# A split product before the second values half: reordering the opening of each step of a fused attention and feed-forward kernel

## The chip, the cores and the metric

The kernel runs on one core of a Trainium2 chip. The metric is device time in microseconds (us), median of several executions. Medians, ranges and ratios below are of executions of the fast state. Ratios are computed as the mean time of one kernel's fast runs over that of the other's fast runs in the same rounds, so they are not quite the ratios of the medians that are quoted beside them; the interval after a ratio is its 95% interval.

## The reference, cut to what matters

```python
def _attn_ref(q, k, v):                 # 8 batches, 8 heads, 576 tokens, head size 64
    k_p = k.reshape(B, H, Sp, 8, D).mean(axis=3)      # keys and values pooled by 8
    v_p = v.reshape(B, H, Sp, 8, D).mean(axis=3)
    attn = softmax(scale * q @ k_p.T)
    return attn @ v_p
def _moe_ref(x, w_in, w_out):           # x: 4608 x 512, w_in: 512 x 2048
    return gelu_tanh(x @ w_in) @ w_out
```

The output of the attention is the input x of the feed-forward part.

## The kernel before

The kernel works in nine steps: one for 512 tokens of each batch, and one ("the remainder") for the 64 left-over tokens of all eight. While TensorE runs the feed-forward part of step g, the attention of step g+1 is woven into it by "hooks": `at(hooks, s, f, ...)` puts the call of f ahead of the matmul numbered s. The attention of one step runs in this order: scores on TensorE, their exponentials ("exps") on ScalarE, the softmax sums on VectorE, transfers on the sync queue that transpose the result into the tile eT, and the values on TensorE, which are copied into the tile xT. xT is what the first product of the next step reads. Hooks 0 to 63 lie in the first product (w_in), 64 to 175 in the second (w_out).

From the fourth step on both products save work by a Strassen-like scheme. Half of the first product is done with seven quarter products ("split products") of 8 matmuls, 128x256 each; two PSUM tiles, x4 and y4, collect sums of products, and in-between sums (partials k2, k0, k1) are copied out to SBUF while later products go on adding into the same tile. The second product has seven output products of 16 matmuls.

```python
def hidden_fast(g, hook):                            # before; cut
    t1, t2, t3, t4 = x_sums(g)                       # needs all of xT
    hidden_two(g, hook)                              # two plain products, need all of xT
    product(x4, 1, A(0, 0), X(0, 0), 8)              # X(h, c): tokens c to c+255 only
    k2 = osb_tile()...
    nc.scalar.copy(out=k2, in_=x4)
    product(y4, 1, A(1, 0), X(1, 0), 12)
    add(out=k2, in0=y4, in1=k2, op=ALU.add)          # add = VectorE
    hidden(g, 2, hook, 16)
    gelu(0, 0, k2)
    product(x4, 0, S(2), T(t2), 20)
    k0, k1 = k2, spare
    nc.scalar.copy(out=k0, in_=x4)
    product(y4, 1, S(1), T(t1), 24)
    nc.scalar.copy(out=k1, in_=y4)
    ...
```

The tail of a step: output products, with the values (attention times V) of the next step in two halves of 256 tokens.

```python
for n, (prod, acc, fresh) in enumerate([(1,xs,1), (2,y,1), (5,z,1), (6,xs,0), (7,xs,0), (3,z,0), (4,xs,0)]):
    ...   # after 1, 6: ScalarE copies xs out; after 5: k2 += y; after 7: k1 += xs; after 3: k0 += z, then store
at(hooks, 64 + 84,  pool, ..., 5, 9)     # VectorE sums of the next values, behind product 7
at(hooks, 64 + 100, values, n, 0)        # within product 4
at(hooks, 64 + 107, values, n, 1)
def osb_tile():
    return work.tile([128, 2, DM], F32, name="osb")  # two buffers, used in turn
```

The softmax here doesn't subtract the row's maximum and nothing guards it: scores larger than these inputs give would overflow.

Of the kernel before, what the change touches and what calls it, by code (L numbers as in the profile page):

```python
# [8 lines left out]
F32 = mybir.dt.float32  # L9
BF16 = mybir.dt.bfloat16  # L10
ALU = mybir.AluOpType
# [8 lines left out]
def kernel(  # L20
# [21 lines left out]
    nc = tc.nc  # L42
# [10 lines left out]
    R = B  # L53
# [265 lines left out]
    BIG = [(64, 0), (0, 1), (64, 1), (0, 2), (0, 3), (64, 3), (0, 4), (64, 4)]  # L319
    SMALL = [(0, 1), (64, 1), (0, 2), (64, 2), (96, 2), (32, 3), (96, 3), (32, 4)]  # L320

    def values(g, half):

        xo = psum.tile([128, HP, 256], F32, name="xo", tag="sc", bufs=2)
        eT, t0 = st[g]["eT"], 256 * half
        for part, rows_ in ((SMALL, 32), (BIG, 64)):
            for pr in range(HP):
                for hh in range(2):
                    r0, c = part[2 * pr + hh]
                    n = dict(PARTS[pr])[c]  # L330
                    nc.tensor.matmul(out=xo[64 * hh:64 * hh + 64, pr, :],  # L331
                                     lhsT=vbd[r0:r0 + rows_, g, n, 64 * hh:64 * hh + 64],
                                     rhs=eT[r0:r0 + rows_, 2 * half:2 * half + 2, c, :],
                                     start=(part is SMALL and pr % 2 == 0), stop=(part is BIG), skip_group_check=True)
        for i, eng in enumerate((nc.scalar, nc.vector)):
            copy(eng, st[g]["xT"][:, 2 * i:2 * i + 2, t0:t0 + 256], xo[:, 2 * i:2 * i + 2])

    def values_r(g):

        xo = [psum.tile([128, 2, MAIN], F32, name="xo", tag="sc", bufs=2) for _ in range(2)]  # L340
        eT = st[g]["eT"]
        for i in range(2):
            for pr in (2 * i, 2 * i + 1):
                for b in range(B):
                    p0 = 64 * (b % 2)
                    for x, (c, n) in enumerate(PARTS[pr]):
                        nc.tensor.matmul(out=xo[i][:, pr % 2, 64 * b:64 * b + 64], lhsT=vbd[:, b, n, :],
                                         rhs=eT[:, b // 2, c, p0:p0 + 64], start=(x == 0), stop=(x == 1))
            copy((nc.scalar, nc.vector)[i], st[g]["xT"][:, 2 * i:2 * i + 2], xo[i])

    def store(g, r, osb, c0=0, c1=DM, eng=nc.sync):
        if g < B:
# [43 lines left out]
    def osb_tile():  # L396
        return work.tile([128, 2, DM], F32, name="osb")
# [38 lines left out]
    def x_sums(g):  # L436

        tt = work.tile([128, 4, 5, 128], BF16, name="tt", tag="eT", bufs=1)
        t1, t2, t3, t4 = t = [tt[:, i, 0:4, :].rearrange("p (i a) b -> p i (a b)", i=2) for i in range(4)]
        x = st[g]["xT"].rearrange("p (h i) t -> p h i t", h=2)  # L440
        b11, b12, b21, b22 = [x[:, h, :, c:c + 256] for h in range(2) for c in (0, 256)]
        for out, in0, in1 in ((t1, b12, b11), (t2, b22, t1), (t3, b22, b12), (t4, b21, t2)):
            nc.vector.tensor_tensor(out=out, in0=in0, in1=in1, op=ALU.subtract)
        return t

    def hidden_fast(g, hook):

        t1, t2, t3, t4 = x_sums(g)
        y, x = [psum.tile([128, 2, MAIN], F32, name="c2", tag="sc", bufs=2) for _ in range(2)]
        y4, x4 = [c.rearrange("p b (m t) -> p (b m) t", m=2) for c in (y, x)]  # L450
        xt = st[g]["xT"].rearrange("p (h i) t -> p h i t", h=2)
        add = nc.vector.tensor_tensor

        def product(acc, fresh, lhs, rhs, s):
            for m in range(4):
                for i in range(2):
                    if i == 0:
                        hook(s + m)
                    nc.tensor.matmul(out=acc[:, m, :], lhsT=lhs(i, m), rhs=rhs(i), start=bool(fresh and i == 0 and m % 2 == 0),  # L459
                                     stop=(i == 1), skip_group_check=True)  # L460

        def A(h, e):
            return lambda i, m: wi[:, h, i, MQ + m, e, :]

        def S(n):
            return lambda i, m: ws[:, n - 1, i, m, :]

        def X(h, c):
            return lambda i: xt[:, h, i, c:c + 256]

        def T(t):
            return lambda i: t[:, i, :]

        def gelu(e, c, src):
            nc.scalar.activation(out=gq[:, MQ:MQ + 4, e, c:c + 256], in_=src, func=ACT.Gelu_apprx_tanh)  # L475

        hidden_two(g, hook)
        product(x4, 1, A(0, 0), X(0, 0), 8)
        k2 = osb_tile().rearrange("p b (m t) -> p (b m) t", m=2)
        nc.scalar.copy(out=k2, in_=x4)  # L480
        product(y4, 1, A(1, 0), X(1, 0), 12)
        add(out=k2, in0=y4, in1=k2, op=ALU.add)
        hidden(g, 2, hook, 16)
        gelu(0, 0, k2)
        product(x4, 0, S(2), T(t2), 20)
        k0, k1 = k2, spare
        nc.scalar.copy(out=k0, in_=x4)  # L487
        product(y4, 1, S(1), T(t1), 24)
        nc.scalar.copy(out=k1, in_=y4)
        hidden(g, 3, hook, 28)  # L490
        product(x4, 0, S(3), T(t3), 32)
        add(out=k1, in0=x4, in1=k1, op=ALU.add)  # L492
        hidden(g, 12, hook, 36)
        gelu(1, 256, k1)
        product(y4, 0, S(4), X(1, 256), 40)
        add(out=k0, in0=y4, in1=k0, op=ALU.add)
        product(x4, 0, A(1, 1), T(t4), 44)
        gelu(1, 0, x4)
        gelu(0, 256, k0)
        for i, fo in enumerate((13, 14, 15)):  # L500
            hidden(g, fo, hook, 48 + 4 * i)
        for i in range(60, 64):
            hook(i)

# [7 lines left out]
        for f in range(2):  # L512
            nc.scalar.activation(out=gT[:, f, :], in_=hp[f], func=ACT.Gelu_apprx_tanh)

    def mlp(g, hooks, last, fast):
        hook = runner(hooks)
        if fast:
            hidden_fast(g, hook)
        else:
            hidden_two(g, hook)  # L520
            for fo in range(2, FO):
                hidden(g, fo, hook, 4 * fo)
# [28 lines left out]

        add = nc.vector.tensor_tensor
        lhs = {1: (gq, 0, 0), 2: (gq, 1, 0), 4: (gq, 1, 256), 5: (gq, 0, 256)}
        for n, (prod, acc, fresh) in enumerate([(1, xs, 1), (2, y, 1), (5, z, 1), (6, xs, 0), (7, xs, 0), (3, z, 0), (4, xs, 0)]):
            for p in range(2):
                for m in range(NP):
                    hook(64 + 16 * n + 8 * p + m)
# [195 lines left out]
    def tail_of_attention(hooks, n, va):  # L753
        at(hooks, va, xT_tile, n)
        at(hooks, va, nc.scalar.preload_act_table_set, GELU_SET)
        at(hooks, va, values, n, 0)
        at(hooks, va, values, n, 1)

    hooks = {}
    at(hooks, 16, first_t, 2)  # L760
# [45 lines left out]
    for n_, g in enumerate(seq):  # L806
# [4 lines left out]
        if n_ == 1:  # L811
            for i in range(1, 4):
                at(hooks, i, w_sums, i, 0, NP, nc.vector)
            at(hooks, 36, g_sums, 0, 4)
            at(hooks, 57, g_sums, 4, 6)
        elif fast:
            at(hooks, 45, g_sums, 0, 2, (0,))
            at(hooks, 57, g_sums, 2, 6, (0,))
            at(hooks, 65, g_sums, 6, 8, (0,))
            at(hooks, 65, g_sums, 0, 8, (1,))  # L820
        else:
            at(hooks, 20, g_sums, 0, 2)
            at(hooks, 36, g_sums, 2, 4)
            at(hooks, 57, g_sums, 4, 6)
        if not fast:
            at(hooks, 65, g_sums, 6, 8)
        if n_ + 1 < len(seq):
# [16 lines left out]
                at(hooks, t1, spread_v, b, nc.gpsimd)  # L844
                at(hooks, 56, k_spread, b, [nc.vector, nc.vector])
            elif kv:
                at(hooks, 4, pool, b, 0, 5, (0,))
                at(hooks, 16, pool, b, 0, 5, (1,))
                at(hooks, 16, dup_k, b, 0, 5)
                at(hooks, 16, kT_tile, b, None)  # L850
                at(hooks, 16, k_transpose_dma, b)
                at(hooks, 16, spread_gated, b)
                at(hooks, 40, k_spread, b, [nc.gpsimd, nc.gpsimd])
            if fast:
                sc_at = [76, 76, 100, 100]
                norm_at = [84, 88, 106, 106]
            else:
                sc_at = [68, 68, 94, 94]
                norm_at = [81, 97, 104, 114]
            for j in range(4):  # L860
                at(hooks, sc_at[j], scores, n, j)
                at(hooks, sc_at[j], exps, n, j)
            at(hooks, norm_at[0], eT_tile, n)
            if fast:
                for j in (2, 3):
# [2 lines left out]
                at(hooks, norm_at[j], norm, n, j, nc.gpsimd if j == 1 else nc.vector)  # L868
                at(hooks, norm_at[j], e_transpose_dma, n, j)
            at(hooks, 64 + 66, nc.scalar.preload_act_table_set, GELU_SET)  # L870
            if n == R:
                at(hooks, 64 + 105, xT_tile, n)
                at(hooks, 64 + 105, values_r, n)
            else:
                at(hooks, 64 + 100, xT_tile, n)
                at(hooks, 64 + 100, values, n, 0)
                at(hooks, 64 + 107, values, n, 1)
        if n_ + 2 < len(seq):
            n2 = seq[n_ + 2]
# [3 lines left out]
            at(hooks, 64 + 52, cast_gated, n2)  # L883
            if n_ >= 2 and n2 != B - 1:
                at(hooks, 64 + 84, pool, B - 1 if n2 == R else n2, 5, 9)
            at(hooks, 64 + 100, qT_tile, n2)
            at(hooks, 64 + 100, q_transpose_dma, n2)
            if n_ == 1:
                at(hooks, 45, load_kv, n2, (0,))
                at(hooks, 64 + 100, load_kv, n2, (1,))  # L890
            else:
                at(hooks, 28, load_kv, n2)
        mlp(g, hooks, n_ + 1 == len(seq), fast)


# [28 lines left out]
```

## Time and profile before

| | before |
|---|---|
| median | 290.24 us (290.11 to 291.05, 3 runs) |
| profiled execution | 291.53 us, span 289.8 us |
| busy: TensorE, VectorE, ScalarE | 94%, 77%, 62% |
| the steps, between exp table loads | 30.09, 29.42, 30.12, 29.40, 29.84, 29.23 us |

The last row is a handy ruler: ScalarE loads the exp table once in each step, just after the first output product has begun, so the gaps between these loads are step lengths.

Here is the timeline view of the kernel before at the end of a step (start us, length us, engine, line, operation, output and input, count, and in brackets how long the engine had been idle and for whom). L587 is the sum into partial k0 of the second product, the first L402 its store, L480 the copy of the first partial k2 in the next step.

```profile
170.15 0.68 DVE L587 TENSOR_TENSOR osb<-mm,osb 128x512 f32<-128x512 f32 x1
...
170.85 0.36 SPq L402 DMA_DIRECT2D out_dram<-osb  x1
...
174.60 1.01 ACT L480 COPY osb<-c 128x1024 f32<-128x1024 f32 x1 [0.22 <-PE c L459]
```

The store lands about 3.1 us after its issue. The copy, which overwrites the stored buffer, waited only for its matmuls (PE).

### The profile page before, as it was taken

The numbers are of one execution on the slowest core, as the hardware profiler recorded it, in microseconds if no ns is written. First come the engines' busy times: TensorE is split into PE (matmuls) and PEld (weight loads), VectorE is DVE, ScalarE is ACT, GpSimd is POOL, SyncE is SP. The second block draws the span as 40 slices with busy tenths as digits, with TensorE's granted clock in tenths as the row PEclk, the third lists the DMA queues.
The fourth block names the chain that finished last, engine by engine and source line by source line (L and its number), as shares of the span: only waits on it lengthen the run. The fifth ranks groups of instructions, "written<-read, shape, count | busy, mean of one in ns | idle before, by whom it ended". The sixth has DMA issues, their size and how long they took to land.

```text
span 289.8 us, 6546 instructions
## 1 busy us (share of the span) xinstructions
PE 273.5 (94%) x2668; PEld 191.7 (66%) x2686; DVE 223.3 (77%) x371; ACT 178.5 (62%) x264; POOL 61.8 (21%) x103
## 2 busy tenths in 40 slices
PE   8899999999999999999899999999999999999994
PEld 3678844447744776767567766775667876766683
DVE  5886779999777989699868997898789538953841
ACT  1596574697356845785379537962886278637820
POOL 4730353003400340404030213123221200100000
PEclk9999999999999999999999999999999999999999
DMA  7999999999989995695659866996651730163013
GB/s 228 303 195 289 375 386 216 315 271 296 163 181 233 354 184 135 168 347 134 148 126 302 210 133 156 307 181 149 162 149 27 174 111 2 25 131 84 2 38 110
DMA packets 71761, 54.37 MB, mean 188 GB/s; under 512 B 45618, under 2 KB 57906, under 8 KB 71730
## 3 DMA queue, kind: packets, MB, share of 16 engines
q1 hardware_dynamic: 69474, 51.72, 69.9%
q0 software_dynamic: 2112, 2.10, 4.5%
q8 instruction: 21, 0.34, 0.5%
q10 hardware_dynamic: 144, 0.13, 0.1%
q14 instruction: 10, 0.08, 0.1%
HBM read 36.70 MB, written 9.44 MB: 159 GB/s over the span
## 4 chain that ended last, share of the span: by engine, by line
PE 73%; ACT 8%; DVE 7%; DMA 7%; issue 2%; SPq 1%; POOL 0%; DVEq 0%
PE mm L565 28%; PE mm L370 16%; PE c L459 9%; PE mm L510 5%; PE mm L381 5%; DMA eT<-eb 3%; PE xo L331 3%; PE x L565 2%; ACT gT L475 2%; ACT osb L487 2%; PE sc L244 2%; DMA q_sb<-in_q_dram 2%; DMA qT<-q_b 1%; ACT osb L92 1%; DVE den L260 1%
## 5 line engine op out<-in xcount | busy, mean ns | idle before, releaser
L370 PE MATMUL mm<-xT,w_in_b 128*128 128x512 bf16 x248 | 58.1, 379 | 0.4
L565 PEld LDWEIGHTS <-gT 128*128 128x128 bf16 x512 | 47.9, 98 | 9.9 <-issue 2.4
L372 ACT ACTIVATE gT<-mm 128x512 bf16<-128x512 f32 x64 | 36.9, 601 | 13.6 <-PE mm L370 13.5
L565 PEld LDWEIGHTS <-stage 128*128 128x128 bf16 x384 | 37.5, 98 | 10.2 <-issue 5.9
L370 PEld LDWEIGHTS <-w_in_b 128*128 128x128 bf16 x256 | 25.1, 98 | 25.1
L92 ACT CAST xT<-xo 128x512 bf16<-128x512 f32 (+1 forms) x17 | 10.4, 610 | 39.2 <-PE xo L331 33.5
L565 PE MATMUL mm<-tw,gT 128*128 128x256 bf16 x240 | 31.8, 273 | 0.0
L565 PE MATMUL mm<-tw,stage 128*128 128x256 bf16 x224 | 26.7, 272 | 4.7 <-ACT osb L92 4.7
L172 POOL TENSOR_TENSOR vbd<-kvb,vmask 128x256 bf16<-128x256 bf16 (+2 forms) x40 | 22.0, 573 | 36.8 <-DVE kvb L152 30.7
L253 ACT ACTIVATE e<-sc 128x576 f32<-128x576 f32 x36 | 22.4, 650 | 10.9 <-PE sc L244 5.8
L565 PE MATMUL mm<-w_out_b,gT 128*128 128x256 bf16 x240 | 29.1, 273 | 0.0
L260 DVE TENSOR_REDUCE den<-e 128x8 f32<-128x576 f32 x36 | 26.1, 735 | 2.3 <-ACT e L253 2.3
L149 DVE TENSOR_TENSOR kv<-kv 128x1024 f32<-128x1024 f32 (+3 forms) x19 | 22.8, 1203 | 3.7 <-DMA kv<-in_k_dram 2.5
L92 ACT COPY osb<-mm 128x512 f32<-128x512 f32 x30 | 17.6, 587 | 13.1 <-PE mm L565 12.0
L459 PEld LDWEIGHTS <-ws 128*128 128x128 bf16 x192 | 18.7, 98 | 7.9 <-issue 2.6
L275 POOL TENSOR_TENSOR eb<-e,r 128x576 bf16<-128x576 f32 x7 | 8.0, 1149 | 73.9 <-DVE r L269 62.9
L275 DVE TENSOR_TENSOR eb<-e,r 128x576 bf16<-128x576 f32 x25 | 20.3, 811 | 0.9
L94 POOL CAST q_b<-q_sb 128x1024 bf16<-128x1024 f32 (+1 forms) x15 | 16.6, 1124 | 20.1 <-DMA q_sb<-in_q_dram 20.1
L94 DVE CAST xT<-xo 128x512 bf16<-128x512 f32 (+1 forms) x17 | 12.2, 720 | 10.1 <-ACT xT L92 6.5
L459 PE MATMUL c<-tt,ws 128*128 128x256 bf16 x144 | 17.7, 272 | 0.9
L492 DVE TENSOR_TENSOR stage<-c,stage 128x1024 f32<-128x1024 f32 x6 | 7.3, 1224 | 13.8 <-PE c L459 13.8
L459 PEld LDWEIGHTS <-w_in_b 128*128 128x128 bf16 x144 | 14.1, 98 | 2.9
(105 smaller groups left out, 438.7 us busy)
## 6 DMA issues: line engine op xcount, KB each, us to landing
kv<-in_k_dram SPq DMA_DIRECT2D x7, 1024.0 KB, 7.1
q_sb<-in_q_dram SPq DMA_DIRECT2D x7, 1024.0 KB, 10.1
kv<-in_v_dram SPq DMA_DIRECT2D x6, 1024.0 KB, 8.1
out_dram<-osb SPq DMA_DIRECT2D x12, 512.0 KB, 3.0
kv<-in_v_dram SPq DMA_DIRECT2D x4, 512.0 KB, 10.1
w_in_b<-in_moe_w_in_dram POOLq DMA_DIRECT2D x4, 512.0 KB, 6.7
w_out_s<-in_moe_w_out_dram SPq DMA_DIRECT2D x2, 1024.0 KB, 13.7
stage<-in_moe_w_out_dram SPq DMA_DIRECT2D x2, 1024.0 KB, 14.8
```

The lines of the kernel that those rows point to most:

```text
L92: eng.copy(out=out, in_=in_)
L94: eng.tensor_copy(out=out, in_=in_)
L149: add(out=t[:, :, 0:4, :], in0=t[:, :, 0:4, :], in1=t[:, :, 4:8, :], op=ALU.add)
L172: eng.tensor_tensor(out=vbd[p0:128, b, n0:n1, :].rearrange("p (c r) (hh d) -> p c (r hh) d", c=max(m, 1), d=D), in0=kvb[p0:128, 4 + c0:4 + ...
L253: nc.scalar.activation(out=e.rearrange("p (x h) s -> p x (h s)", x=2), in_=sc[:, :, 0:4 * Sp], func=ACT.Exp, scale=1.0 / 64.0)
L260: nc.vector.reduce_sum(out=den, in_=e, axis=AX.X)
L275: eng.tensor_tensor(out=o.rearrange("p (pr hh s) -> p hh pr s", hh=2, s=Sp), in0=e.rearrange("p (hh pr) s -> p hh pr s", hh=2), in1=r.rear ...
L370: nc.tensor.matmul(out=hp, lhsT=w_in_b[:, ko, fo * 128:(fo + 1) * 128], rhs=st[g]["xT"][:, ko, :], start=(i == 0), stop=(i == KO - 1))
L372: nc.scalar.activation(out=gT[:, fo, :], in_=hp, func=ACT.Gelu_apprx_tanh)
L381: nc.tensor.matmul(out=hp[:, f, :], lhsT=w_in_b[:, ko, (fo + f) * 128:(fo + f + 1) * 128], rhs=st[g]["xT"][:, ko, c0:c0 + 256], start=(ko ...
L459: nc.tensor.matmul(out=acc[:, m, :], lhsT=lhs(i, m), rhs=rhs(i), start=bool(fresh and i == 0 and m % 2 == 0), stop=(i == 1), skip_group_ch ...
L565: nc.tensor.matmul(out=xs[p] if acc is xs else acc[:, p, :], lhsT=lt, rhs=rt, start=bool(fresh and m == 0 and (p == 0 or (last and acc is ...
```

## The change

The intent: a step should open with work that needs only the first half of the tokens, so that TensorE need not wait for the second values half and its copy; the copy of partial 6 should lie beside a product that does not use its bank; and ScalarE should be relieved of one copy. Some other work is moved to make room. The core of the diff (cut):

```diff
-        hidden_two(g, hook)
-        product(x4, 1, A(0, 0), X(0, 0), 8)
-        k2 = osb_tile()...
+        product(x4, 1, A(0, 0), X(0, 0), 0)
+        rest()                                  # values(g, 1), copied by ScalarE and VectorE
+        (t1, t2, t3, t4), make = x_sums(g)
+        make(1, 2)
+        k2, k0, k1 = part(), part(), spare      # part() = osb_tile(), so two buffers now
         nc.scalar.copy(out=k2, in_=x4)
-        product(y4, 1, A(1, 0), X(1, 0), 12)
+        product(y4, 1, A(1, 0), X(1, 0), 4)
         add(out=k2, in0=y4, in1=k2, op=ALU.add)
+        make(3, 4)
+        hidden(g, 0, hook, 8)
+        hidden(g, 1, hook, 12)
+        product(x4, 0, S(2), T(t2), 16)
+        nc.scalar.copy(out=k0, in_=x4)
 ...
-        nc.scalar.copy(out=k1, in_=y4)
+        nc.vector.tensor_copy(out=k1, in_=y4)
 ...
-        enumerate([(1, xs, 1), (2, y, 1), (5, z, 1), (6, xs, 0), (7, xs, 0), (3, z, 0), (4, xs, 0)])
+        enumerate([(1, xs, 1), (2, y, 1), (6, xs, 0), (5, z, 1), (7, xs, 0), (3, z, 0), (4, xs, 0)])
 ...
-                at(hooks, 4, pool, b, 0, 5, (0,))
+                at(hooks, 64 + 98, pool, B - 1 if n2 == R else n2, 0, 5, (0,))     # one step earlier
-                at(hooks, sc_at[j], exps, n, j)
+                at(hooks, max(sc_at[j], 80), exps, n, j)
-                at(hooks, 64 + 107, values, n, 1)                                  # kept for two early steps
```

The transfer that transposes q also moves, from hook 164 to hook 2 of the next step, behind the last output store.

More of the change, by code (lines that the diff above doesn't have):

```diff
@@ L320, with values @@
     SMALL = [(0, 1), (64, 1), (0, 2), (64, 2), (96, 2), (32, 3), (96, 3), (32, 4)]
-    def values(g, half):
-        xo = psum.tile([128, HP, 256], F32, name="xo", tag="sc", bufs=2)
+    def values(g, half, split=True):
         eT, t0 = st[g]["eT"], 256 * half
-        for part, rows_ in ((SMALL, 32), (BIG, 64)):
-            for pr in range(HP):
-                for hh in range(2):
-                    r0, c = part[2 * pr + hh]
-                    n = dict(PARTS[pr])[c]
-                    nc.tensor.matmul(out=xo[64 * hh:64 * hh + 64, pr, :],
-                                     lhsT=vbd[r0:r0 + rows_, g, n, 64 * hh:64 * hh + 64],
-                                     rhs=eT[r0:r0 + rows_, 2 * half:2 * half + 2, c, :],
-                                     start=(part is SMALL and pr % 2 == 0), stop=(part is BIG), skip_group_check=True)
-        for i, eng in enumerate((nc.scalar, nc.vector)):
-            copy(eng, st[g]["xT"][:, 2 * i:2 * i + 2, t0:t0 + 256], xo[:, 2 * i:2 * i + 2])
@@ L338, in values_r @@
-    def values_r(g):
-        xo = [psum.tile([128, 2, MAIN], F32, name="xo", tag="sc", bufs=2) for _ in range(2)]
-        eT = st[g]["eT"]
-        for i in range(2):
-            for pr in (2 * i, 2 * i + 1):
-                for b in range(B):
+        if half == 0 or not split:
+            xo = psum.tile([128, HP, 256], F32, name="xo", tag="sc", bufs=2)
+            dst = [xo[:, pr, :] for pr in range(HP)]
+        else:
+            xo = [psum.tile([128, 2, 256], F32, name="xo", tag="mm", bufs=4) for _ in range(2)]
+            dst = [xo[pr // 2][:, pr % 2, :] for pr in range(HP)]
@@ new lines, in values @@
+        if g < B:
+            for part, rows_ in ((SMALL, 32), (BIG, 64)):
+                for pr in range(HP):
+                    for hh in range(2):
+                        r0, c = part[2 * pr + hh]
+                        n = dict(PARTS[pr])[c]
+                        nc.tensor.matmul(out=dst[pr][64 * hh:64 * hh + 64],
+                                         lhsT=vbd[r0:r0 + rows_, g, n, 64 * hh:64 * hh + 64],
+                                         rhs=eT[r0:r0 + rows_, 2 * half:2 * half + 2, c, :],
+                                         start=(part is SMALL and pr % 2 == 0), stop=(part is BIG), skip_group_check=True)
+        else:
+            for pr in range(HP):
+                for b in range(4):
@@ L345, in values_r @@
                     p0 = 64 * (b % 2)
                     for x, (c, n) in enumerate(PARTS[pr]):
-                        nc.tensor.matmul(out=xo[i][:, pr % 2, 64 * b:64 * b + 64], lhsT=vbd[:, b, n, :],
-                                         rhs=eT[:, b // 2, c, p0:p0 + 64], start=(x == 0), stop=(x == 1))
-            copy((nc.scalar, nc.vector)[i], st[g]["xT"][:, 2 * i:2 * i + 2], xo[i])
+                        nc.tensor.matmul(out=dst[pr][:, 64 * b:64 * b + 64], lhsT=vbd[:, 4 * half + b, n, :],
+                                         rhs=eT[:, 2 * half + b // 2, c, p0:p0 + 64], start=(x == 0), stop=(x == 1))
@@ L351, in store @@
+        xT = st[g]["xT"]
+        if half == 0 or not split:
+            copy([nc.scalar, nc.vector][half], xT[:, :, t0:t0 + 256], xo)
+        else:
+            for i, eng in enumerate((nc.scalar, nc.vector)):
+                copy(eng, xT[:, 2 * i:2 * i + 2, t0:t0 + 256], xo[i])
     def store(g, r, osb, c0=0, c1=DM, eng=nc.sync):
@@ L441, in x_sums, with make, hidden_fast @@
         b11, b12, b21, b22 = [x[:, h, :, c:c + 256] for h in range(2) for c in (0, 256)]
-        for out, in0, in1 in ((t1, b12, b11), (t2, b22, t1), (t3, b22, b12), (t4, b21, t2)):
-            nc.vector.tensor_tensor(out=out, in0=in0, in1=in1, op=ALU.subtract)
-        return t
-    def hidden_fast(g, hook):
-        t1, t2, t3, t4 = x_sums(g)
+        def make(*which):
+            for w in which:
+                out, in0, in1 = ((t1, b12, b11), (t2, b22, t1), (t3, b22, b12), (t4, b21, t2))[w - 1]
+                nc.vector.tensor_tensor(out=out, in0=in0, in1=in1, op=ALU.subtract)
+        return t, make
+    def hidden_fast(g, hook, rest):
         y, x = [psum.tile([128, 2, MAIN], F32, name="c2", tag="sc", bufs=2) for _ in range(2)]
@@ L475, in gelu, with part @@
             nc.scalar.activation(out=gq[:, MQ:MQ + 4, e, c:c + 256], in_=src, func=ACT.Gelu_apprx_tanh)
-        hidden_two(g, hook)
-        product(x4, 1, A(0, 0), X(0, 0), 8)
-        k2 = osb_tile().rearrange("p b (m t) -> p (b m) t", m=2)
+        def part():
+            return osb_tile().rearrange("p b (m t) -> p (b m) t", m=2)
+        product(x4, 1, A(0, 0), X(0, 0), 0)
[3 more added lines that the diff above has]
+        k2, k0, k1 = part(), part(), spare
         nc.scalar.copy(out=k2, in_=x4)
-        product(y4, 1, A(1, 0), X(1, 0), 12)
+        product(y4, 1, A(1, 0), X(1, 0), 4)
         add(out=k2, in0=y4, in1=k2, op=ALU.add)
-        hidden(g, 2, hook, 16)
-        gelu(0, 0, k2)
-        product(x4, 0, S(2), T(t2), 20)
-        k0, k1 = k2, spare
-        nc.scalar.copy(out=k0, in_=x4)
-        product(y4, 1, S(1), T(t1), 24)
-        nc.scalar.copy(out=k1, in_=y4)
-        hidden(g, 3, hook, 28)
-        product(x4, 0, S(3), T(t3), 32)
+        make(3, 4)
[3 more added lines that the diff above has]
+        nc.scalar.copy(out=k0, in_=x4)
+        gelu(0, 0, k2)
+        product(y4, 1, S(1), T(t1), 20)
+        nc.vector.tensor_copy(out=k1, in_=y4)
+        hidden(g, 2, hook, 24)
+        product(x4, 0, S(3), T(t3), 28)
         add(out=k1, in0=x4, in1=k1, op=ALU.add)
-        hidden(g, 12, hook, 36)
+        hidden(g, 3, hook, 32)
         gelu(1, 256, k1)
-        product(y4, 0, S(4), X(1, 256), 40)
+        product(y4, 0, S(4), X(1, 256), 36)
         add(out=k0, in0=y4, in1=k0, op=ALU.add)
-        product(x4, 0, A(1, 1), T(t4), 44)
+        product(x4, 0, A(1, 1), T(t4), 40)
         gelu(1, 0, x4)
         gelu(0, 256, k0)
-        for i, fo in enumerate((13, 14, 15)):
-            hidden(g, fo, hook, 48 + 4 * i)
+        for i, fo in enumerate((12, 13, 14, 15)):
+            hidden(g, fo, hook, 44 + 4 * i)
         for i in range(60, 64):
@@ L513, in hidden_two, with mlp @@
             nc.scalar.activation(out=gT[:, f, :], in_=hp[f], func=ACT.Gelu_apprx_tanh)
-    def mlp(g, hooks, last, fast):
+    def mlp(g, hooks, last, fast, rest=None):
         hook = runner(hooks)
         if fast:
-            hidden_fast(g, hook)
+            hidden_fast(g, hook, rest)
         else:
@@ L553, in mlp @@
         lhs = {1: (gq, 0, 0), 2: (gq, 1, 0), 4: (gq, 1, 256), 5: (gq, 0, 256)}
-        for n, (prod, acc, fresh) in enumerate([(1, xs, 1), (2, y, 1), (5, z, 1), (6, xs, 0), (7, xs, 0), (3, z, 0), (4, xs, 0)]):
+        for n, (prod, acc, fresh) in enumerate([(1, xs, 1), (2, y, 1), (6, xs, 0), (5, z, 1), (7, xs, 0), (3, z, 0), (4, xs, 0)]):
             for p in range(2):
@@ L756, in tail_of_attention @@
         at(hooks, va, values, n, 0)
-        at(hooks, va, values, n, 1)
+        at(hooks, va, values, n, 1, False)
     hooks = {}
@@ L816 @@
         elif fast:
-            at(hooks, 45, g_sums, 0, 2, (0,))
+            at(hooks, 41, g_sums, 0, 2, (0,))
             at(hooks, 57, g_sums, 2, 6, (0,))
@@ L846 @@
             elif kv:
-                at(hooks, 4, pool, b, 0, 5, (0,))
-                at(hooks, 16, pool, b, 0, 5, (1,))
-                at(hooks, 16, dup_k, b, 0, 5)
-                at(hooks, 16, kT_tile, b, None)
-                at(hooks, 16, k_transpose_dma, b)
-                at(hooks, 16, spread_gated, b)
+                at(hooks, 17, pool, b, 0, 5, (1,))
+                at(hooks, 17, dup_k, b, 0, 5)
+                at(hooks, 17, kT_tile, b, None)
+                at(hooks, 17, k_transpose_dma, b)
+                at(hooks, 17, spread_gated, b)
                 at(hooks, 40, k_spread, b, [nc.gpsimd, nc.gpsimd])
             if fast:
+                at(hooks, 2, qT_tile, n)
+                at(hooks, 2, q_transpose_dma, n)
                 sc_at = [76, 76, 100, 100]
@@ L870 @@
             at(hooks, 64 + 66, nc.scalar.preload_act_table_set, GELU_SET)
-            if n == R:
-                at(hooks, 64 + 105, xT_tile, n)
-                at(hooks, 64 + 105, values_r, n)
-            else:
-                at(hooks, 64 + 100, xT_tile, n)
-                at(hooks, 64 + 100, values, n, 0)
+            at(hooks, 64 + 100, xT_tile, n)
+            at(hooks, 64 + 100, values, n, 0)
+            if n_ < 2:
                 at(hooks, 64 + 107, values, n, 1)
@@ L885 @@
                 at(hooks, 64 + 84, pool, B - 1 if n2 == R else n2, 5, 9)
-            at(hooks, 64 + 100, qT_tile, n2)
-            at(hooks, 64 + 100, q_transpose_dma, n2)
+                at(hooks, 64 + 98, pool, B - 1 if n2 == R else n2, 0, 5, (0,))
+            if n_ < 2:
+                at(hooks, 64 + 100, qT_tile, n2)
+                at(hooks, 64 + 100, q_transpose_dma, n2)
             if n_ == 1:
@@ L892 @@
                 at(hooks, 28, load_kv, n2)
-        mlp(g, hooks, n_ + 1 == len(seq), fast)
+        mlp(g, hooks, n_ + 1 == len(seq), fast, lambda: values(g, 1))
 _INS = ['q', 'k', 'v', 'moe_w_in', 'moe_w_out']
```

## The prediction

> **What bounds the kernel now.** I first read the busy shares and the granted clock on the page.
>
> ```profile
> PE 273.5 (94%) x2668; PEld 191.7 (66%) x2686; DVE 223.3 (77%) x371; ACT 178.5 (62%) x264; POOL 61.8 (21%) x103
> PEclk9999999999999999999999999999999999999999
> ```
>
> TensorE is busy 94% at full clock, so it is the bound; removing work from another engine pays only where TensorE waits for it. Next, who TensorE (PE) waited for, over the whole span (columns: who, for what; total us, times, longest).
>
> ```profile
> PE mm L565 <- ACT osb L92: 4.7, 7, 0.7
> PE xo L331 <- DMA eT<-eb: 1.5, 2, 0.9
> ```
>
> L565 is the output product, L331 the values product. The chain of waits, in order of time, shows where the rest sits, here in the fifth step (start us, length, what).
>
> ```profile
> 171.00 0.15 PE xo L331 x4
> 171.15 0.02 issue
> 171.17 0.59 ACT xT L92
> 171.76 0.04 issue
> 171.81 0.38 PE mm L510
> ...
> 175.44 0.88 PE mm L370 x4
> 176.32 0.02 issue
> 176.34 0.60 ACT gT L372
> 176.94 1.04 ACT gT L475
> 177.97 0.02 issue
> 178.00 1.02 ACT osb L487
> 179.02 0.04 issue
> 179.06 1.03 PE c L459 x8
> ...
> 193.30 0.59 ACT osb L92
> 193.89 0.04 issue
> 193.94 1.92 PE mm L565 x16
> ```
>
> Three things hold TensorE: the copy of the second values half into xT before the step opens; the ScalarE copy of partial k0 before the third split product; and the copy of partial 6 before product 7, which accumulates in the same bank. Last, the windows view cut at each step's first hidden product.
>
> ```profile
> 142.41:171.81 29.40, 28.28 (x295) 20.54 (x297) 25.26 (x41) 19.49 (x28) 6.77 (x12) 1.00 0.78 190
> 171.81:201.65 29.84, 28.28 (x294) 20.55 (x296) 25.32 (x41) 19.47 (x28) 8.11 (x12) 1.00 0.93 201
> ```
>
> Columns after the length are PE, PEld, DVE and ACT busy. DVE has 25.3 us of work in 29.5, so it has little room if the step shrinks to 28.
>
> **What the Trainium skill says.** "TensorE: Matmul & The Clock Gate", Back-to-back issue gap: warm, N/2.4 + 2.5 ns, so 109 ns for 256 columns. The trace agrees: 16 such take 1.75 us (109 ns), four of 512 take 0.87. So true work is count times 109 ns, and the 28.28 "busy" overstates it. "VectorE: DVE Perf Modes", Why PSUM operands drop a tier: fp32 from PSUM runs at one element per cycle, so the moved 128x1024 copy gains nothing; the trace's like-sized operations from PSUM take 1.22 us on VectorE and 1.01 on ScalarE. "DMA: Bandwidth & Descriptors", Anatomy of one DMA: a transfer signals only after its last byte is confirmed, with a fixed part of about 2 us. The 512 KB output stores here take 3.0 us from issue to landing, and I will need that.
>
> **The change, part by part.** TensorE's work per step: 8 hidden products x 0.866 = 6.93, 7 split products x 0.872 = 6.10, 7 output products x 1.745 = 12.2, scores 0.77, values 1.40: 27.4 us. The five middle steps last 29.55 on average (260.06 - 112.29 = 147.8).
>
> 1. Output products run as 1,2,6,5,7 instead of 1,2,5,6,7. The copy of partial 6 (0.59) now lies beside product 5 (1.75). This removes the 0.67 wait in seven steps: -4.7 us. For product 6 to come earlier, the copy of partial 1 must be done when product 2 ends; the exps moved to hook 80 let it go first on ScalarE. This delays the first exps by 0.6, but VectorE reached their sums only at 189.39, when both had been done for 0.7, so nothing is lost.
> 2. The second half of the values moves behind the first quarter product. The opening no longer needs xT's second half. This removes the 0.22 opening gap in six steps (-1.3), and the wait for the last transposed eT, because it now has about 12 matmuls of product 4 and 8 of the quarter product before it. From product 1 to the next opening the steps take 16.63, 15.91, 16.36, against 15.69 undisturbed: 0.94 + 0.22 + 0.67 = -1.8. The first half is copied by ScalarE alone (128x1024, 1.02) beside 12 remaining matmuls (1.31): it just fits.
> 3. The split phase takes 13.49 us in each of six steps, its work is 13.03. With two hidden products between the k2 copy and the next product, and k1 copied by VectorE, the 0.3 wait (178.76 to 179.06) and small ones go: up to -2.7 in all.
>
> Ideal sum: 4.7 + 1.3 + 1.8 + 2.7 = 10.5, so 279.8.
>
> Costs. k0 now has a buffer of its own, so k2 and k0 take the two osb buffers that the last two output stores still read. Before, the first of these stores was issued at 170.85 and landed 3.1 later (173.95), 0.65 before k2 was written at 174.60. Now the order on VectorE is x_add, pooling of the next values (3.0 us under the GpSimd casts), k0 add, and this kept the k0 add until 4.54 us after product 7 (166.29 to 170.83). Product 3, product 4 and one values half take 1.75 + 1.75 + 0.79 = 4.29. So the store is issued about 0.1 to 0.3 us after the new opening (T) and lands at T+3.2 to T+3.4. k2 could have been copied at T+2.2. It ends near T+4.3, its add near T+5.5, and the product that rewrites that bank, due at T+5.1, waits 0.4; VectorE then does two sums (0.8), the pooling stage of hook 17 (1.6) and its new k1 copy (1.2), reaching the k1 add late. I estimate 0.6 us in each of four steps: +2.4. The last step follows the one with stores in eight pieces; the pieces behind k0 cost +0.7. One step issues its transposes late behind eight q loads (+0.5), and ScalarE's queue of gelus at the end of the split phase costs +0.3 to 0.5. Costs 4.0; estimate 279.8 + 4.0 = 283.8. As the costs are guessed at their full size and the gains are read off, I put the centre a little lower, at 283.4.
>
> **Rivals.** (a) Store wait harmless: if k0's add comes earlier on VectorE (its chain of normalisations starts 0.4 to 0.7 earlier, as I work it out from ScalarE's queue), the store lands by T+2.5 and the time is near 281. For it: x_add itself waited 0.2 for TensorE. Against: it can start no earlier than product 7's end, and the pooling still stands before the add. (b) VectorE becomes the bound: it keeps 25.3 us, gains 1.2 (k1) and loses 0.7 (xT), 25.8 in a 28 us step. In-order waits on top would make every step 28.7 and the time 286 to 287. For: the chain already passes through a VectorE add and pooling before the eT transfer at 196. Against: 2 us of slack. (c) The transposes set the pace: eT's last one landed 14.3 to 15 us after product 1; the new values half is due at 14.9. Against: at most 0.1 to 0.6 in one or two steps; 284 to 285. (d) Transfers of q and the pools collide with the new order, slower than now: nothing in the waits speaks for it, as removed waits are worth 10.
>
> **Range and chances.** The order of output products alone is nearly certain (1.6%); 2% needs 284.4 and my centre is 1 us below it. Range 280.3 to 287.0. Faster by over 2%: 0.62, within: 0.37, slower: 0.01.
>
> **What would show it.** PE's waits: "mm L565 <- ACT osb" gone (right for 1). No wait on eT before the values and none before the opening product (2). The middle steps 27.9 to 28.6 apart. If my cost is right, the k2 copy on ScalarE waits on an out_dram store, starting near T+3.3, and PE waits on VectorE's k2 or k1 add; if it starts at T+2.2, rival (a). PE waits on VectorE in all steps, also those without a late store, would be (b). Wrong outright: step lengths still above 29, or the 0.67 wait come back before product 6.

(What it calls the fifth step, opening at 171.81, is the sixth of the nine, counted from the first.)

## The result, and the profile after

The changed kernel took 285.42 us (285.06 to 285.56, 4 runs) against 290.51, ratio 0.9822 [0.9801, 0.9842]; a second measurement of it, with more rounds, gave 285.05 us and 0.9786 [0.9763, 0.9809]. So the gain is right at 2%. The time lay inside the predicted range, 2.0 us above its centre.

First the view of whom TensorE waited for, in the changed kernel (who, for what; total us, times, longest). L466 is a split product, L492 the copy of k2, L494 the sum into k2, L505 the sum into k1, L337 the values.

```profile
PE c L466 <- ACT osb L492: 0.9, 2, 0.6
PE c L466 <- DVE stage L505: 0.6, 3, 0.2
PE xo L337 <- DMA eT<-eb: 0.5, 1, 0.5
PE c L466 <- DVE osb L494: 0.5, 2, 0.2
```

The 4.7 us for the copy of partial 6 are gone, as intended. New are waits of the split products on the partials. What those waited for stands in the same view over all engines:

```profile
ACT osb L492 <- DMA out_dram<-osb: 4.2, 4, 1.7
...
ACT osb L499 <- DMA out_dram<-osb: 1.6, 2, 0.9
```

ScalarE waits for output stores before it may copy k2 (L492) and k0 (L499). The chain of waits of the changed kernel, at the opening of the fifth step (start us, length, what), shows where that leads:

```profile
138.93 0.69 DVE osb L600
139.63 0.02 issue
139.64 3.28 DMA out_dram<-osb
...
143.00 1.02 ACT osb L492
144.02 0.02 issue
144.04 1.22 DVE osb L494
145.27 0.67 DVE tt L450 x2
145.94 0.74 DVE kv L151
...
147.49 1.14 DVE stage L502
...
148.75 1.23 DVE stage L505
149.98 0.04 issue
150.02 1.03 PE c L466 x8
```

The step opens at 139.32. The sum into k0 (L600) ends at 139.61, its store lands at 142.9, the k2 copy starts at 143.00, 3.7 us after the opening. Then VectorE has several things to do in order, among them the new k1 copy (L502), and TensorE gets its seventh product's bank back only at 150.0. Between one L600 and the next, the chain passes through TensorE's last hidden products, the exps, VectorE's softmax sums and the pooling to the next L600. Read so, it is a closed loop through VectorE, a transfer and ScalarE, and where it is closed the step is as long as the loop (the next two experiments cut it): the k2 copies of two consecutive steps start at 113.95 and 143.00, 29.05 us apart.

The windows view over that step, in the changed kernel (span from start to end; length; then busy us of PE, PEld, DVE, ACT and POOL; clock; DMA share; GB/s):

```profile
126.12:155.16 29.04, 28.21 (x297) 20.50 (x297) 25.93 (x42) 19.16 (x26) 7.84 (x12) 1.00 0.75 198
```

The step lengths after are 29.41, 29.55, 29.04, 28.45, 28.57, 28.09.

### The profile page after: what moved, and what is told of

It reads as the page before. It is cut to its first block, busy times and chain, and to the rows that moved or that the text cites. A ratio compares the mean times of both kernels' runs of the same rounds, so it can differ in the third digit from the quotient of the medians.

```text
span 283.7 us, 6524 instructions
## 1 busy us (share of the span) xinstructions
PE 272.1 (96%) x2668; PEld 191.7 (68%) x2686; DVE 226.0 (80%) x370; ACT 176.8 (62%) x258; POOL 64.3 (23%) x103
## 4 chain that ended last, share of the span: by engine, by line
PE 62%; DVE 22%; DMA 8%; issue 3%; ACT 2%; POOL 1%; SPq 1%; DVEq 0%; ACTq 0%; POOLq 0%
PE mm L578 21%; PE mm L374 18%; PE c L466 8%; PE mm L385 5%; DVE den L260 4%; DMA out_dram<-osb 3%; DVE eb L275 3%; DVE kv L151 3%; PE x L578 2%; PE xo L337 2%; DMA q_sb<-in_q_dram 2%; DVE kv L149 2%; PE sc L244 2%; DMA qT<-q_b 2%; DVE stage L505 1%
## 5 line engine op out<-in xcount | busy, mean ns | idle before, releaser
L374 PE MATMUL mm<-xT,w_in_b 128*128 128x512 bf16 x290 | 68.1, 379 | 0.7
L376 ACT ACTIVATE gT<-mm 128x512 bf16<-128x512 f32 x76 | 43.6, 599 | 13.2 <-PE mm L374 12.6
L374 PEld LDWEIGHTS <-w_in_b 128*128 128x128 bf16 x304 | 29.8, 98 | 30.7
L92 ACT CAST xT<-xo 128x512 bf16<-128x512 f32 (+1 forms) x17 | 13.4, 787 | 31.7 <-PE xo L337 26.8
L578 PE MATMUL mm<-tw,gT 128*128 128x256 bf16 x240 | 30.0, 273 | 0.0
L578 PE MATMUL mm<-tw,stage 128*128 128x256 bf16 x224 | 27.6, 273 | 0.0
L466 PEld LDWEIGHTS <-ws 128*128 128x128 bf16 x192 | 18.8, 98 | 8.5 <-issue 2.9
L94 POOL CAST q_b<-q_sb 128x1024 bf16<-128x1024 f32 (+1 forms) x15 | 19.3, 1304 | 19.7 <-PE mm L385 14.2
L149 DVE TENSOR_TENSOR kv<-kv 128x1024 f32<-128x1024 f32 (+3 forms) x19 | 21.0, 1105 | 3.1 <-DMA kv<-in_k_dram 1.9
L466 PE MATMUL c<-tt,ws 128*128 128x256 bf16 x144 | 18.1, 272 | 1.5 <-ACT osb L492 0.9
L94 DVE CAST xT<-xo 128x512 bf16<-128x512 f32 (+1 forms) x10 | 7.4, 744 | 11.8 <-PE xo L337 6.4
L426 DVE TENSOR_TENSOR stage<-gT 128x512 bf16<-128x512 bf16 (+1 forms) x25 | 13.6, 546 | 4.1 <-ACT gT L482 2.5
L466 PEld LDWEIGHTS <-w_in_b 128*128 128x128 bf16 x144 | 13.6, 98 | 3.6 <-issue 2.1
```

What stands on the lines that cost most here:

```text
L92: eng.copy(out=out, in_=in_)
L94: eng.tensor_copy(out=out, in_=in_)
L149: add(out=t[:, :, 0:4, :], in0=t[:, :, 0:4, :], in1=t[:, :, 4:8, :], op=ALU.add)
L374: nc.tensor.matmul(out=hp, lhsT=w_in_b[:, ko, fo * 128:(fo + 1) * 128], rhs=st[g]["xT"][:, ko, :], start=(i == 0), stop=(i == KO - 1))
L376: nc.scalar.activation(out=gT[:, fo, :], in_=hp, func=ACT.Gelu_apprx_tanh)
L466: nc.tensor.matmul(out=acc[:, m, :], lhsT=lhs(i, m), rhs=rhs(i), start=bool(fresh and i == 0 and m % 2 == 0), stop=(i == 1), skip_group_ch ...
```

## The experiments

All outputs are right. "Before" was timed on the same chip; the median of its fast executions was 291.4 to 291.5 us there, with single ones from 290.6 to 294.1.

### Partials in memory of their own

k2 and k0 go to a part of the stage tile that lies idle then, so that no store has to be awaited.

```diff
-        k2, k0, k1 = part(), part(), spare
+        k2, k0, k1 = stage[:, 0:1024]..., stage[:, 2048:3072]..., spare   # a helper's slices, written out
```

> k2 and k0 are put in the part of the stage tile that is idle then (the sums of the output product), so no partial waits for an output store any more. Theory A (the k0 add stands behind the pooling on VectorE, its store lands at about T+3.3, the k2 copy waits for it, and VectorE and then TensorE follow): the waits of ScalarE on out_dram stores (4.2 + 1.6 us) go, the first three fast steps shrink from 29.6, 29.0, 28.4 to about 28.0 to 28.3, and the time is 282.0 to 283.5. Rival B (VectorE simply has too much work for a 28 us step): the wait goes but VectorE stays busy end to end, the steps keep their length, 284.9 to 285.8.

Measured: 282.31 us, 0.9679 [0.9643, 0.9715]. The windows view of three steps of this run:

```profile
124.49:152.33 27.84, 27.84 (x299) 20.51 (x297) 26.05 (x42) 18.94 (x27) 6.77 (x12) 1.00 0.77 207
152.33:180.16 27.83, 27.83 (x299) 20.52 (x297) 26.04 (x42) 18.93 (x26) 6.83 (x12) 1.00 0.83 205
180.16:209.59 29.43, 27.90 (x299) 20.57 (x297) 25.91 (x42) 18.94 (x26) 7.02 (x12) 1.00 0.91 190
```

In the first two steps TensorE is busy for the whole length: nothing is left to wait for. VectorE does 26.05 us of work in 27.84, the same work as in the 29.04 us step above. So VectorE's amount of work was not the bound; its place in the loop behind the store was. The third step has a new wait, 1.5 us for the transposed eT; below.

### The sum into k0 ahead of the pooling

```diff
-                at(hooks, 64 + 84, pool, B - 1 if n2 == R else n2, 5, 9)
+                at(hooks, 64 + 96, pool, B - 1 if n2 == R else n2, 5, 9)
```

> The pooling of the second half of the next values is moved behind the k0 add; the work of VectorE is the same, in another order. Theory A: the k0 add ends about 2.6 us earlier, the store lands before T+1, the k2 copy no longer waits; part of it is lost because the pooling now stands before the xT copy and the k2 add in the opening: 282.5 to 284.5. Rival B: as VectorE does the same work in the same steps, 284.9 to 285.8.

Measured: 282.76 us, 0.9702 [0.9665, 0.9739]. One number of the diff cures nearly as much as the memory of its own. The timeline of this run at the opening of the fourth step:

```profile
107.23 0.69 DVE L600 TENSOR_TENSOR osb<-mm,osb 128x512 f32<-128x512 f32 x1 [0.69 <-PE mm L578]
...
111.83 1.02 ACT L492 COPY osb<-c 128x1024 f32<-128x1024 f32 x1
```

The sum now waits for nothing but its product, and the k2 copies no longer wait for a store (two of the k0 copies still do, for 0.8 and 0.7 us, and TensorE does not wait for them). The step lengths are 29.44, 28.04, 27.83, 27.83, 28.98, 28.09. There is a second effect: before, the pooling ran beside GpSimd's casts of q, now behind them. The 128x512 addition of the pooling takes 0.69 us here against 1.41 in the changed kernel, and two casts take 2.02 instead of 3.04; the 128x1024 addition just before it takes 1.22 in both. So the run changes two things, the place of the sum and this overlap; the run with own memory, which still has the pooling beside the casts, is the cleaner proof. The Trainium skill, "GPSIMD Engine Reference", Specifications, says that GpSimd shares its SBUF interface with VectorE and that VectorE instructions with two SBUF inputs contend for it; the trace agrees, for one of these two additions, and gives the size.

### The order of the output products alone, with the later exps

The kernel before with two of the change's lines:

```diff
-        enumerate([(1, xs, 1), (2, y, 1), (5, z, 1), (6, xs, 0), ...
+        enumerate([(1, xs, 1), (2, y, 1), (6, xs, 0), (5, z, 1), ...
-                at(hooks, sc_at[j], exps, n, j)
+                at(hooks, max(sc_at[j], 80), exps, n, j)
```

> The kernel before with only the order of the output products (6 before 5) and the exps behind the copy of partial 1. By step 1 of the prediction it gives -4.7 us: 285.5 to 286.2, so about the whole measured gain, and the split part would be worth nothing net. Rival: with the 0.67 wait gone another wait (the transposed eT, the exps) takes its place at once and it gives 2 to 3 us only, 287.5 to 288.5.

Measured: 294.27 us (292.93 to 295.39, the 4 fast executions of 6; the other two, 297.7 and 298.6, had a granted clock of 0.982), 1.0089 [1.0039, 1.0138]. Both expectations were wrong: it is slower than before. TensorE waited 6.5 us in five places for the transposed eT. The next two runs take the two lines apart. Neither line alone makes the kernel measurably slower; why both together do stays open. The lower clock of some executions (0.992 to 0.994 in three of the four fast ones) may have a part in it.

### The later exps alone, and the order alone

> The kernel before with only the exps moved behind the copy of partial 1 (in two steps of the eight they move from hook 68 to 80). If the later exps are what kept the order alone from paying: slower than before by 0.5 to 2 per cent, TensorE waiting longer for the transposed eT. If they are harmless, as the prediction said: within 0.3 per cent of before.

Measured: 292.54 us, 1.0023 [0.9985, 1.0062]. Not distinguishable from before. The sign of harm that was named did appear, though: in its profiled execution, the longest of the six, TensorE waited 3.3 us for eT, against 1.5 before. So a small loss, within the interval, is not excluded.

> The kernel before with only the order of the output products. Theory C: TensorE reaches the values 0.6 us earlier and waits for eT instead: within 0.5 per cent of before, the 0.67 waits gone or smaller (product 6 now waits some 0.6 us for the copy of partial 1, which comes behind two exps) and the waits on eT up from 1.5 us. Theory of the harmful exps: 286 to 288, as step 1 of the prediction had it.

Measured: 291.44 us (289.60 to 293.51, 5 fast executions of 6), 1.0000 [0.9950, 1.0049]. The waits of TensorE in this run:

```profile
PE xo L331 <- DMA eT<-eb: 3.0, 4, 1.7
PE xo L347 <- DMA eT<-eb: 2.2, 1, 2.2
```

The 4.7 us of the kernel before on the copy of partial 6 are no longer listed, and no wait of product 6 on the copy of partial 1 has come up (I had expected 0.6 each). In their place are 5.2 us on eT, against 1.5 before. The chain of waits of this run shows what TensorE stood before (start us, length, what): the last transposed eT, behind VectorE's softmax sums.

```profile
131.89 0.76 DVE eb L275
...
134.49 4.31 DMA eT<-eb
138.80 0.14 issue
138.93 0.81 PE xo L331 x16
```

TensorE came 0.67 us earlier to a gate that did not open earlier. By these waits 3.7 of the 4.7 us were handed to the other wait; the rest is too little to show in the ratio, whose interval is half a per cent wide to either side. Three of the five fast executions had a lower clock (0.993 or 0.994); the two at 0.999 or more took 289.60 and 291.04 us, so a gain of about a microsecond may be hidden there, but not one of 4.7.

### The changed kernel with the old order

The order line undone, everything else as changed.

> The changed kernel with the old order of the output products (5 before 6); the deferred values half stays. Theory C (the two halves pay only together: the new order makes TensorE arrive earlier, the deferred values half is what keeps it from waiting for the transposed eT there): the 0.67 wait is back in seven steps; in the three steps that the late store holds, part of it is hidden behind that loop: 287 to 289.5. Prediction's view (the parts add up): 285.4 + 4.7 = 290.1. Rival: the order is worth nothing anywhere, as alone: 285.4.

Measured: 288.86 us, 0.9913 [0.9893, 0.9934]. TensorE waits for the copy of partial 6 again, in seven places:

```profile
PE mm L578 <- ACT osb L92: 4.7, 7, 0.7
```

So the order that was worth nothing measurable alone is worth 3.8 us or 1.3% here (0.9913 against 0.9786 of the changed kernel).

### The changed kernel with the second values half back in the tail

```diff
-            if n_ < 2:
-                at(hooks, 64 + 107, values, n, 1)
+            at(hooks, 64 + 107, values, n, 1)
-        mlp(g, hooks, n_ + 1 == len(seq), fast, lambda: values(g, 1))
+        mlp(g, hooks, n_ + 1 == len(seq), fast, lambda: None)
```

> The changed kernel with the second half of the values back before the step's end; the order of products, the quarter products that open the step and everything else stay. Theory C: TensorE waits for the transposed eT again in most fast steps, by 1 to 2.3 us as in the run with the order alone: 289 to 293. If only the late store matters (theory A without C): the values half sits elsewhere but TensorE has the same work, 285 to 286.

Measured: 287.14 us (286.41 to 289.01), 0.9865 [0.9836, 0.9895], less bad than expected. TensorE's waits in this run:

```profile
PE xo L337 <- DMA eT<-eb: 2.4, 3, 1.1
PE c L466 <- ACT osb L492: 1.4, 2, 1.1
```

The wait on eT is back in three steps, and the loop over the store is still there. Both the transposes and the store hold TensorE, in different steps, and the deferred half takes most of the first away (2.4 us here, 0.4 and 0.5 in the two profiles of the changed kernel). With the half back in the tail the kernel is still over 1% faster than before, though. No run has the changed kernel with both the old order and the half in the tail, so how much of the order's worth hangs on the deferral, and how much on the rest of the change, is not shown.

### The changed kernel unaltered

> The changed kernel itself, unaltered, so that the other runs of this call have it on the same chip: 285.0 to 286.0.

Measured: 285.05 us, 0.9786 [0.9763, 0.9809]. Its step lengths, in a second profile, are 29.70, 29.55, 28.41, 28.45, 28.94, 28.09.

### k1 copied by ScalarE again

```diff
-        nc.vector.tensor_copy(out=k1, in_=y4)
+        nc.scalar.copy(out=k1, in_=y4)
```

> k1 copied by ScalarE again, everything else as changed. Theory A: ScalarE reaches that copy only after the k0 copy and one gelu, so it ends about when VectorE's ends now; VectorE gets 1.2 us back in each step but the loop over the late store stays: 285.0 to 286.5. Rival B: 1.2 us less on VectorE in each of six steps shortens them by up to that, 281 to 283.5.

Measured: 284.83 us, 0.9770 [0.9736, 0.9805]. That is 0.2 us below the expected range; no difference from the changed kernel can be claimed, so as to time the copy by VectorE is worth nothing. The steps tell more: 29.40, 29.27, 28.06, 28.10, 29.87, 28.17. The third and fourth, 28.06 and 28.10, had been 29.04 and 28.45 in the first profile of the changed kernel and 28.41 and 28.45 in the second; so 1.2 us of VectorE's work less seems to shorten the loop, by 0.35 to 1.0, against what I expected. This is one profile, and the two of the changed kernel differ by 0.6 in the third step themselves, so it is not shown. The fifth, 28.57 and 28.94 there, lost about what was gained, as it now waited 1.4 for eT.

### The step that waits for eT whenever the rest is fast

Around the start of the fifth of these intervals the queries of the 64 left-over tokens of each batch are loaded in eight transfers of 128 KB with small packets. With the partials in their own memory that step took 29.43 us. Three runs start from that kernel. Half of these loads issued by GpSimd:

```diff
-                eng.dma_start(out=t[p0:p0 + 64, :, b // 2, :], in_=...)
+                (eng if b < 4 else nc.gpsimd).dma_start(out=t[p0:p0 + 64, :, b // 2, :], in_=...)
```

> The run with partials in their own memory, and in addition half of the eight q loads for the remainder step issued from GpSimd, as they keep the sync queue until 187.2 and so the transposes of that step back (the one step there that takes 29.4 instead of 27.8, with 1.5 us of TensorE waiting for eT). If that is the cause: that step 28.0 to 28.3, 280.8 to 281.6. If the transposes are slow for the traffic itself: 282.3, the same step again 29.4.

Measured: 284.06 us (282.68 to 285.47), 0.9749 [0.9712, 0.9786], which is above both expectations; three of its six executions had a clock of 0.993 or 0.994 and took 284.9 to 285.5, the other three 282.7 to 283.2. The step again 29.34. The first transpose was issued at 184.94 instead of 187.18, yet all four were issued by 193.1 against 193.6. The Trainium skill, "DMA: Bandwidth & Descriptors", Issuing engines are not separate DMA queues, says that transfers from all issuers end up on the same 16 engines and only issue time is saved; this fits it.

The loads earlier, ahead of those of k and v:

```diff
-            s2 = 44 if n_ == 1 else 30 if n2 == R else 57
+            s2 = 44 if n_ == 1 else 18 if n2 == R else 57
```

> The run with partials in their own memory, the eight q loads of the remainder step issued before the loads of k and v instead of behind them. The traffic of their small packets then ends some 2 us earlier, before the transposes of that step: its length falls from 29.4 to 28.0 to 28.8 and the time to 281.0 to 282.0. If the k and v loads then collide with the transposes in their place: 282.3 or more.

Measured: 282.80 us (281.71 to 285.65), 0.9696 [0.9650, 0.9743]; the step 29.51. The k and v loads now stood right ahead of the transposes. What exactly slows the transposes in that step, where the 16 engines are 0.91 busy, stays open; neither of the two changes to the order of issue shortened it. In this last run the four were issued from 184.52 on, 2.7 us earlier, but took 7.90 us to issue, and the slowest landed after 7.5.

The exps at their old places:

```diff
-                at(hooks, max(sc_at[j], 80), exps, n, j)
+                at(hooks, sc_at[j], exps, n, j)
```

> The run with partials in their own memory, exps at their old places. The copy of partial 1 comes 1.2 us later and product 6 waits for it, about 0.5 us in each fast step: 283.5 to 285.5 against 282.3. If VectorE gains more from the earlier exps than TensorE loses: 281 to 282.

Measured: 281.92 us, 0.9658 [0.9621, 0.9694]. No wait of product 6 came up. The move of the exps is worth nothing that these runs can tell. This run and the first of this section are the best versions found, some 1% faster than the change and over 3% faster than before; their order is within the intervals.

### The parts side by side

| kernel | ratio to before |
|---|---|
| before + order of products | 1.0000 |
| before + later exps | 1.0023 |
| before + both | 1.0089 |
| changed, old order | 0.9913 |
| changed, second values half in the tail | 0.9865 |
| changed | 0.9786, 0.9822 |
| changed, k1 by ScalarE | 0.9770 |
| changed, k0 sum ahead of the pooling | 0.9702 |
| changed, partials in own memory | 0.9679 |
| the same, exps early | 0.9658 |

## Why the prediction was right or wrong

**The range held, the most likely class is at its border.** 283.4 was predicted, with 62% for more than 2% faster; measured were 1.8% and 2.1%.

**The base was mismatched.** The prediction read its gains from the profiled execution and subtracted them from the median. That execution was 291.53 us, 1.3 above the median. In the profiles the span fell from 289.8 to 283.7, by 6.1; in the medians by 5.1. From 291.5 the ideal sum of 10.5 leads to 281.0, not 279.8. The run without the store wait comes near that figure: 282.9 in its profiled execution, less the 1.5 it waited for eT, is 281.4.

**Step 1, "nearly certain", was wrong as it stood.** The wait of 0.67 was real and the new order removes it. But the order alone gave no measurable gain where 4.7 us were forecast, as TensorE then stands before eT. The prediction added steps 1 and 2 as if independent. They are not: on top of the rest of the change, the deferral with it, the order is worth 3.8 us. That the deferral is what makes it pay is the likely reading, as it takes the eT waits away, but it was not isolated. The sum came out well because the parts were made together; as the prediction had not seen that they must be, this was luck. Its remark that the later exps were needed was wrong too: with the old exps no such wait appears.

**Step 2 was right in kind.** No wait before the opening product; eT is waited for in one step, 0.5 us (the predicted +0.5). Undoing the deferral alone costs 2.1 us. The first values half, copied by ScalarE alone, did fit beside the rest of product 4.

**Step 3 was right.** Without the store wait the steps are 27.83 to 27.84 us with TensorE busy throughout, so the split phase had no gaps left (the prediction's sum of TensorE's work in a step, 27.4, is 0.4 short of this). The k1 copy by VectorE had no measurable part in it.

**The cost was the right mechanism with wrong sizes.** Every link that the prediction named is in the chain above. The k2 copy, put at near T+3.3, started at T+4.0 in the first such step (113.95 against an opening at 109.94) and T+3.7 in the next. Measured against the run with own memory the steps lost 1.54, 1.20 and 0.62 us (29.55 - 28.01, 29.04 - 27.84, 28.45 - 27.83), 3.4 in all, and 2.7 by the second profile of the changed kernel, where 0.6 in each of four steps was put down. It is more in the first steps, none in the last. Two intervals, 29.55 and 29.04, even met the prediction's own sign for "wrong outright", step lengths above 29; the store wait, not the missing gains, is what kept them there, as the run with own memory has 28.01 and 27.84. I had costed one delay of TensorE, not a loop that comes round: a late k0 sum makes the next step's VectorE work late, and so the next k0 sum. The fifth interval shows no loss against that run (28.57 against 29.43), since there eT would have held TensorE anyway.

**Two costs did not appear.** The stores in eight pieces held the last step's k2 copy for 0.5 us, but not TensorE: the interval into it is 27.83 us long (239.62 to 267.45 on the chain). ScalarE's queue of gelus, put at 0.3 to 0.5, is not seen in the run with own memory, where the steps are TensorE throughout.

**Rivals.** (a) did not come: the store wait was not harmless. A cure of it gives 282.3, where (a) had said near 281. (b) falls by the windows view: VectorE held the same 26 us in a 27.84 us step. It may have a grain of truth, if the k1 copy lengthens the loop. (c) is right for one step. (d) did not happen.

## What to carry to other kernels

A wait removed ahead of a gate that opens at its own time can be worth nothing; ask what TensorE meets next, and defer the work behind that gate in the same change. When a temporary takes a buffer whose last reader is a store, write down when that store can be issued, and on which engine's queue the work before it stands: one moved line (the sum ahead of the pooling) gave 1%. Subtract gains that were read off a trace from the time of that execution, not from the median.

## What the Trainium skill lacked or had wrong

- "GPSIMD Engine Reference" names the contention with VectorE but gives no times for it: a 128x512 fp32 addition from SBUF took 1.41 us beside the casts and 0.69 after them, and the two 128x1024 casts took 3.04 instead of 2.02.
- "DMA: Bandwidth & Descriptors" gives a rate for the transposing transfer, and what its issue costs only in cycles and for transfers of other shapes. Here each 128x640 transpose took at least 1.2 us of the sync queue, so four of them about 4.9, and landing took 2.6 us at best and 4.2 to 4.3 in several steps.
- No page tells why the mean granted clock of one kernel scatters by one or two per cent, and its time with it: with the order and the exps moved alone, the six executions had clocks of 0.982 to 0.998 and took 292.9 to 298.6 us; the changed kernel had 0.998 or more and took 285.0 to 285.5 in the five of its second measurement. No run here shows what causes it.
- "TensorE: Matmul & The Clock Gate", Back-to-back issue gap: the formula that the prediction used is given there for isolated matmuls. For a sustained stream the section has about 131 ns for each matmul of 512 columns, and says that the formula counts too much. The trace disagrees: four of these in a row take 0.86 us, about 216 ns each, as the formula has it.
